# Row maxima of the segment attention: whole masked rows on VectorE in place of packed blocks

## The chip, the cores and the metric

One NeuronCore of a Trainium2 chip runs the whole program. The metric is device time in microseconds (us), the median of three runs. The engines work side by side: TensorE (PE in the profile; its weight loads are PEld), VectorE (DVE), ScalarE (ACT), GpSimd (POOL) and SyncE (SP, which here only issues transfers).

## The reference, cut to what matters

Two attention layers of 32 heads with 16 dimensions read the same 2048 tokens, and a gate mixes them. Side A is full softmax attention. Side B works on four segments of 512 tokens: causal softmax inside a segment, plus a memory carried from segment to segment. The change is in side B's softmax, in the row maxima that keep the exponential in range:

```python
def _A_ref(x, wqkv, wo):
    ...
    scores = jnp.einsum("bhqd,bhkd->bhqk", q, k) * scale
    p = _softmax(scores, axis=-1)
    o = jnp.einsum("bhqk,bhkd->bhqd", p, v)
    ...
def _B_ref(x, wq, wk, wv, wo, beta):
    B, S, D = x.shape
    H = 32; Dh = D // H; N = 4; L = S // N
    ...
    mask = (lambda x, dt: x.astype(dt))(ar[:, None] < ar[None, :], x.dtype) * (-1e9)
    ...
    for s in range(N):
        qs, ks, vs = q[:, :, s], k[:, :, s], v[:, :, s]
        logits = jnp.einsum("bhqd,bhkd->bhqk", qs, ks) * scale + mask
        p = _softmax(logits, axis=-1)
        a_dot = jnp.einsum("bhqk,bhkd->bhqd", p, vs)
        ...
```

## The kernel before

**Units.** The work of both sides is cut into units of four heads and 512 queries: 32 units of side A and 32 of side B (`NU`). A unit passes twice through TensorE. The first pass (`max_part`, products at L208) computes scores with queries in the partitions, and VectorE takes the maximum of each row. The second pass (`score_part`, products at L660) computes them again with keys in the partitions, with two extra rows of the query tile that carry the negated maximum, so that ScalarE can take the exponential straight from PSUM (L683, L680) and TensorE can multiply by the values (L716).

**Slots.** A unit of side A has 64 slots, one of side B 10 (`SLOTS`). Units alternate, so that a unit of A and one of B, 74 slots together, form the period of the kernel's middle stage. The loop at the end of `gated_mix` makes one slot after another, and this order is the order of each engine's queue. In slot n it emits one second-pass product and its exponential, and one first-pass bank for slot m = n + 96 (`LEAD`). After every third slot (`BURST`) it emits up to five pieces of value products, or eight small products of the output projection, so TensorE's stream comes in bursts: three score products, three first-pass banks, then the values. In the list `maxs` the ten B banks stand seven slots apart among the 64 of A; in the first block with B, and in the last one, which has two units of B, they stand three apart.

**Banks.** The first pass uses four PSUM banks of 128 x 512 in turn. TensorE can write a bank again when whoever read it is done, so it can be at most four slots ahead of its readers. The second pass has three banks (`st_ps`), and the values one.

**First pass of side A.** One product of 48 x 128 by 48 x 512 fills a bank, and one VectorE reduction of 128 x 512 empties it (L223). When the unit is complete, a small reduction joins the parts and negates them (L180).

**First pass of side B.** Queries 128 s to 128 s + 127 need keys 0 to 128 s + 127, the last 128 of these under the causal triangle. The kernel cuts these rows into blocks of 128 keys and packs the blocks so that each of the ten banks of a unit is full, in five kinds for each pair of heads. Kinds 0 and 1 hold four diagonal blocks each (four products of 128 columns): ScalarE copies the bank to SBUF (L234), GpSimd masks the copy (L235), and eight slots later VectorE reduces it (L238; `MASK_T`). Kinds 2 and 3 hold the rest of rows 1 and 3 of one head (products of 128 and 384 columns, reduction at L244), kind 4 the rest of row 2 of two heads (two products of 256, reduction at L248). That is 28 products and ten reductions of 512 columns for a unit. The block maxima go to a tile `pmB` that GpSimd filled with -3.0e38 once (L172 to L174), and a small reduction joins them (L182).

**After the maxima.** `finish_max` (L176) splits the negated maxima on GpSimd into two parts (L187, L188). `transpose_max` (L191) then transposes them on TensorE with four small products (L196), in a bank of the second pass; ScalarE copies the result (L199), and SyncE issues two transfers for each unit into the query tiles (L202). `todo` and `late` hold these steps back by fixed numbers of slots: for side B the small reduction comes 9 slots after the unit's last bank and the transposition 18 slots after it, for side A 0 and 14. Where both are due together, they share one transposition.

**Beside it.** GpSimd also masks the exponentials of side B (L664) and scales finished heads (L779, L781). VectorE also takes reciprocals of the softmax sums (L767) and multiplies them by gates (L769, L771). Ahead of the middle stage lies the projection of queries, keys and values; VectorE's product with a running sum at L467 is there.

Of the kernel before, what the change touches and what calls it, by code (L numbers as in the profile page):

```python
# [10 lines left out]
F32 = mybir.dt.float32  # L11
F32R = mybir.dt.float32r
AF = mybir.ActivationFunctionType
ALU = mybir.AluOpType
AX = mybir.AxisListType
# [7 lines left out]
CH = 512  # L23
NCH = S // CH
KT = D // 128
NG = 8
NO = 4
SCALE = 0.25
MASKED = -1.0e9 / SCALE

# [5 lines left out]
MOST = 3  # L38
NP = 6
GAP = {"A": 3, "B": 5}  # L40
MASK_T = 8
LATE_T = 8
PRE = 20
NKA, NKB = 8, 2
# [3 lines left out]
def gated_mix(ctx, tc, x, xT, wqkv, a_wo, b_wq, b_wk, b_wv, b_wo, beta, gate_w, out):  # L48
    nc = tc.nc
# [7 lines left out]
    for side in "AB":  # L57
        for o in range(NO):
            for c in range(NCH):
# [20 lines left out]
                            compare_op=ALU.not_equal, fill=1.0)  # L80
# [12 lines left out]
    mp = ctx.enter_context(tc.tile_pool(name="mp", bufs=2))  # L93
# [18 lines left out]
    for k in range(NU):  # L112
        mine = {u: iter(range(32)) for u in range(2)}
# [3 lines left out]
        for p in range(64 + 10 * len(bs)):  # L117
            r = (len(maxs) + 1) % 2
            i = (p - start) // apart
# [42 lines left out]
    def rows(t, h, n):  # L162

        return t[64 * (h // 2):64 * (h // 2) + n, h % 2]


    pmt = {}
    todo = []
    late = []


    pmB = [mp.tile([128, 2, 4, 8], F32, name=f"pmB{i}", bufs=1) for i in range(2)]  # L172
    for t in pmB:
        nc.gpsimd.memset(t, -3.0e38)  # L174

    def finish_max(u):  # L176
        nm = mp.tile([128, 4, 4], F32, tag="nm", name="nm")
        pm = pmt.pop(u)
        if u[0] == "A":
            nc.vector.tensor_reduce(nm, pm, axis=AX.X, op=ALU.max, negate=True)  # L180
        else:
            nc.vector.tensor_reduce(nm.rearrange("p h (a b) -> p (h a) b", b=2),  # L182
                                    pm.rearrange("p b h (a k) -> p (h a) b k", a=2), axis=AX.X, op=ALU.max, negate=True)

        ms = mp.tile([128, 2, 2, 2, 4], F32R, tag="ms", name="ms")
        nv = nm.rearrange("p (r h) s -> p r h s", r=2)
        nc.gpsimd.tensor_copy(ms[:, :, 0], nv)  # L187
        nc.gpsimd.tensor_sub(ms[:, :, 1], nv, ms[:, :, 0].bitcast(F32))  # L188
        return ms
# [11 lines left out]
            for r in range(2):  # L201
                nc.sync.dma_start(raw(qt[u])[64 * r + 48:64 * r + 50], raw(mt)[32 * i + 16 * r:32 * i + 16 * r + 16])  # L202

    def blocked(ps):
        return ps.rearrange("p (b t) -> p b t", t=128)

    def max_product(ps, u, h, s, n0, n, k, k0=0):
        nc.tensor.matmul(ps[:, n0:n0 + n], rows(qt[u][:, :, s * 128:(s + 1) * 128], h, 48), rows(k[:, :, k0:k0 + n], h, 48),  # L208
                         start=True, stop=True)

    def max_part(m, bank):

        u, (r, i) = maxs[m]
        side, g, c = u
        if u not in pmt:
            pmt[u] = mp.tile([128, 4, 4, 4], F32, tag="pmA", name="pm") if side == "A" else pmB[(c * NG + g) % 2]
        pm = pmt[u]
        ps = bank()
        if side == "A":

            kc, s, h = i // 8, i % 8 // 2, 2 * r + i % 2
            max_product(ps, u, h, s, 0, CH, kt_[u, kc])
            nc.vector.tensor_reduce(pm[:, h, s, kc:kc + 1], ps, axis=AX.X, op=ALU.max)  # L223
        else:


            k = kt_[u, c]
            h0 = 2 * r
            if i < 2:
                for n in range(4):  # L230
                    b = i + 2 * (n % 2)
                    max_product(ps, u, h0 + n // 2, b, 128 * n, 128, k, 128 * b)
                dg = dp.tile([128, 4, 128], F32, tag="dg", name="dg")
                nc.scalar.copy(dg, blocked(ps))  # L234
                nc.gpsimd.affine_select(out=dg, in_=dg, pattern=[[0, 4], [-1, 128]], base=0, channel_multiplier=1,  # L235
                                        compare_op=ALU.is_ge, fill=MASKED)
                to = pm[:, i, h0:h0 + 2, 3::4] if i == 0 else pm[:, i, h0:h0 + 2, 1::6]
                todo.append((m + MASK_T, lambda: nc.vector.tensor_reduce(  # L238
                    to, dg.rearrange("p (h s) t -> p h s t", h=2), axis=AX.X, op=ALU.max)))
            elif i < 4:  # L240
                h = h0 + i - 2
                max_product(ps, u, h, 1, 0, 128, k)
                max_product(ps, u, h, 3, 128, 384, k)
                nc.vector.tensor_reduce(pm[:, 1, h, 3:7], blocked(ps), axis=AX.X, op=ALU.max)  # L244
            else:
                for f in range(2):
                    max_product(ps, u, h0 + f, 2, 256 * f, 256, k)
                nc.vector.tensor_reduce(pm[:, 0, h0:h0 + 2, 4:6], ps.rearrange("p (h b t) -> p h b t", h=2, b=2), axis=AX.X,  # L248
                                        op=ALU.max)
        if m == last_max[u]:  # L250
            def finish():
                late.append((m + MASK_T + 2 + LATE_T - (4 if side == "A" else 0), u, finish_max(u)))
            todo.append((m + (MASK_T + 1 if side == "B" else 0), finish))

    def run_todo(m):

# [26 lines left out]
    with ExitStack() as p0:  # L283
# [264 lines left out]
        def some_max():  # L548
            m = mnext[0]
            if m == LEAD:  # L550
                return
            loads(m + 3 + PRE)
            for i in range(4):
                max_part(m + i, lambda: me_sm.tile([128, CH], F32, tag="sm", name="sm"))
            run_todo(m + 3)
            mnext[0] += 4
            run_late(me_ps, "me", mnext[0])
# [42 lines left out]
    pp = ctx.enter_context(tc.tile_pool(name="pp", bufs=NP, reuse_waits="tile"))  # L600

    va = ctx.enter_context(tc.tile_pool(name="va", bufs=2, reuse_waits="tile"))
    dp = ctx.enter_context(tc.tile_pool(name="dp", bufs=3, reuse_waits="tile"))
    ob = ctx.enter_context(tc.tile_pool(name="ob", bufs=2, reuse_waits="tile"))
    wo = ctx.enter_context(tc.tile_pool(name="wo", bufs=1, reuse_waits="tile"))
    fr = ctx.enter_context(tc.tile_pool(name="fr", bufs=1, reuse_waits="tile"))
# [28 lines left out]
    for (s, c), t in gate.items():  # L635
        nc.gpsimd.dma_start(t, gd["AB".index(s), c * CH:(c + 1) * CH].rearrange("(q t) -> q t", q=16)
                            .unsqueeze(0).broadcast_to([8, 16, 32]))

    pt_ = {}
    order_p = {}  # L640
# [159 lines left out]
    fill = []  # L800
# [63 lines left out]
    n = 0  # L864
    while n < nS or queue or beside or filled[0] < len(fill):
# [4 lines left out]
        m = n + LEAD  # L870
        if m < nS:
            loads(m + PRE)

            def bank():
                i = free.pop(0)
                free.append(i)
                return banks[i]
            max_part(m, bank)
# [22 lines left out]
    for b in range(4):  # L901
# [3 lines left out]
        t = fr.tile([128, D], F32, tag="vM" if b % 2 else "res", name="res", bufs=2)  # L905
# [4 lines left out]
def build():  # L910
    import concourse.bacc as bacc
    nc = bacc.Bacc("TRN2", target_bir_lowering=False, num_devices=1)
    shapes = {"x": (S, D), "xT": (D, S), "wqkv": (D, 3 * D), "a_wo": (D, D), "b_wq": (D, D), "b_wk": (D, D),
              "b_wv": (D, D), "b_wo": (D, D), "beta": (H,), "gate_w": (D,)}
    args = [nc.dram_tensor(n, s, F32, kind="ExternalInput").ap() for n, s in shapes.items()]
    out = nc.dram_tensor("out", (S, D), F32, kind="ExternalOutput").ap()
    with tile.TileContext(nc) as tc:
        gated_mix(tc, *args, out)
    return nc
# [23 lines left out]
```

## Time and profile before

| | us |
|---|---|
| Median of three runs (lowest to highest) | 1882.79 (1882.19 to 1883.36) |
| The profiled execution's own time | 1883.44 |
| Its span, first to last instruction | 1881.7 |
| Busy in the span: ACT | 1502.9 |
| Busy in the span: POOL | 314.9 |

The profile is of one execution. Its page gives the busy time of each engine and the chain of work that ended last. Views of the trace group instructions by line and shape, list them in order of time, and sum busy time in chosen stretches. "Busy" counts the time in which at least one instruction of the engine was under way, so overlapping instructions count once; the distance from one start to the next tells what an instruction costs its engine in a full queue. Matmul ends are modelled, so a busy TensorE is not the same as one at its peak.

### The profile page before, as it was taken

To read this page: it belongs to the slowest core of one execution; us is meant where nothing else is said; L and a number is where in the kernel's file an instruction comes from. 1 tells how busy PE (TensorE), PEld (TensorE's weight loads), DVE (VectorE), ACT (ScalarE), POOL (GpSimd) and SP (SyncE) were. 2 spreads that over 40 slices of the span, in tenths; PEclk is the share of its full clock that TensorE was granted. 3 is DMA by queue.
4 is the path that set the end of the run, shared out by engine and by line. 5 is a ranking of instruction groups with operands and counts; after the bars stand their busy time and mean duration, and the time that the engine had idled before them with its cause. 6 is when DMAs were issued, how large, how long until landed. Compare 5 with 4: busy or idle time off the path is not lost.

```text
span 1881.7 us, 46459 instructions
## 1 busy us (share of the span) xinstructions
PE 1863.1 (99%) x18153; PEld 1006.1 (53%) x18153; DVE 1596.5 (85%) x2745; ACT 1502.9 (80%) x2900; POOL 314.9 (17%) x515
## 2 busy tenths in 40 slices
PE   9999999999999999999999999999999999999998
PEld 7888676555555454444444444444444454555545
DVE  4235777999999999999999999999999999999820
ACT  5445444898888898888888888888888888888884
POOL 3001222111111111121111111211121211111210
PEclk9999999999999999999999999999999999999999
DMA  7567555234343433343434343434343434343211
GB/s 239 192 231 255 196 184 192 84 115 136 87 109 86 115 91 111 94 117 97 117 92 117 98 113 102 113 98 113 97 113 101 113 103 115 102 114 95 84 57 46
DMA packets 124170, 227.31 MB, mean 121 GB/s; under 512 B 34952, under 2 KB 49960, under 8 KB 123440
## 3 DMA queue, kind: packets, MB, share of 16 engines
q1 hardware_dynamic: 122448, 222.68, 41.1%
q8 instruction: 144, 2.36, 0.5%
q0 software_dynamic: 1216, 1.14, 0.2%
q14 instruction: 74, 0.61, 0.1%
q10 hardware_dynamic: 288, 0.52, 0.1%
HBM read 155.52 MB, written 67.52 MB: 119 GB/s over the span
## 4 chain that ended last, share of the span: by engine, by line
PE 90%; ACT 4%; DMA 3%; DVE 1%; issue 1%; SPq 1%; POOL 1%; ACTq 0%; POOLq 0%; DVEq 0%
PE ops L716 30%; PE st L660 27%; PE sm L208 14%; PE pr L320 11%; PE ops L793 6%; ACT p L683 2%; ACT dg L234 1%; DMA qB<-mt 1%; PE num L502 1%; POOL mn L380 1%; SPq L202 0%; DMA qdB<-q 0%; PE sm L793 0%; PE mps L533 0%; DMA raw<-wqkv 0%
## 5 line engine op out<-in xcount | busy, mean ns | idle before, releaser
L683 ACT ACTIVATE p<-st 128x512 f32<-128x512 f32 x2304 | 1223.4, 605 | 180.8 <-PE sm L208 147.4
L223 DVE TENSOR_REDUCE pm<-sm 128x1 f32<-128x512 f32 x2048 | 1282.9, 683 | 62.1 <-PE sm L208 43.0
L208 PE MATMUL sm<-kA,qA 48*128 48x512 f32 x2048 | 741.5, 445 | 0.0
L660 PE MATMUL st<-qA,kA 50*128 50x512 f32 x2048 | 693.6, 436 | 3.6 <-ACT p L683 3.1
L660 PEld LDWEIGHTS st<-qA,kA 50*128 50x128 f32 x2048 | 332.9, 185 | 436.0 <-ACT p L683 370.6
L716 PE MATMUL ops<-p,vA 128*17 128x512 f32 (+3 forms) x5848 | 556.4, 469 | 0.0
L208 PEld LDWEIGHTS sm<-kA,qA 48*128 48x128 f32 x2048 | 332.5, 184 | 21.1 <-DVE pm L223 7.9
L716 PEld LDWEIGHTS ops<-p,vA 128*17 128x17 f32 x5848 | 109.7, 95 | 174.0 <-issue 152.4
L208 PE MATMUL sm<-kB,qB 48*128 48x128 f32 (+2 forms) x896 | 168.6, 291 | 0.0
L208 PEld LDWEIGHTS sm<-kB,qB 48*128 48x128 f32 x896 | 134.6, 186 | 9.8 <-DVE pm L223 2.8
L235 POOL TENSOR_SCALAR_AFFINE_SELECT dg<-dg 128x512 f32<-128x512 f32 x128 | 81.2, 635 | 289.1 <-ACT dg L234 289.1
L660 PE MATMUL st<-qB,kB 50*128 50x384 f32 (+3 forms) x512 | 120.4, 341 | 2.6 <-DMA qB<-mt 1.2
L187 POOL CAST ms<-nm 128x16 fp32r<-128x16 f32 x64 | 12.6, 196 | 646.6 <-DVE nm L180 401.5
L383 DVE TENSOR_TENSOR q<-full,q 128x512 fp32r<-128x512 f32 x64 | 44.1, 689 | 86.9 <-ACT q L376 86.4
L660 PEld LDWEIGHTS st<-qB,kB 50*128 50x128 f32 x512 | 71.4, 185 | 67.9 <-ACT p L683 47.3
L664 POOL TENSOR_SCALAR_AFFINE_SELECT p<-p 128x512 f32<-128x512 f32 x128 | 78.8, 634 | 95.9 <-ACT p L683 93.9
L244 DVE TENSOR_REDUCE pmB<-sm 128x4 f32<-128x512 f32 x128 | 87.3, 682 | 0.5 <-PE sm L208 0.5
L716 PE MATMUL ops<-p,vB 128*17 128x128 f32 (+3 forms) x1192 | 86.5, 398 | 0.4
L238 DVE TENSOR_REDUCE pmB<-dg 128x4 f32<-128x512 f32 x128 | 86.7, 677 | 0.0
L375 ACT COPY full<-pr 128x512 f32<-128x512 f32 x64 | 37.3, 583 | 52.0 <-PE pr L320 51.8
L234 ACT COPY dg<-sm 128x512 f32<-128x512 f32 x128 | 76.4, 597 | 1.0 <-DVE pmB L238 0.6
L767 DVE RECIPROCAL rec<-rec 128x32 f32<-128x32 f32 x44 | 15.1, 344 | 66.0 <-DMA rec<-odA 35.3
(145 smaller groups left out, 1588.8 us busy)
## 6 DMA issues: line engine op xcount, KB each, us to landing
kA<-kdA SPq DMA_DIRECT2D x256, 128.0 KB
vA<-vdA SPq DMA_DIRECT2D x31, 544.0 KB
kA<-kdA SPq DMA_DIRECT2D x256, 64.0 KB
qdA<-q SPq DMA_DIRECT2D x32, 256.0 KB
kdA<-q SPq DMA_DIRECT2D x32, 256.0 KB
qdB<-q SPq DMA_DIRECT2D x32, 256.0 KB
qA<-qdA SPq DMA_DIRECT2D x64, 128.0 KB
kdB<-q SPq DMA_DIRECT2D x32, 256.0 KB
```

The source lines that it names most:

```text
L208: nc.tensor.matmul(ps[:, n0:n0 + n], rows(qt[u][:, :, s * 128:(s + 1) * 128], h, 48), rows(k[:, :, k0:k0 + n], h, 48), start=True, stop=True)
L223: nc.vector.tensor_reduce(pm[:, h, s, kc:kc + 1], ps, axis=AX.X, op=ALU.max)
L234: nc.scalar.copy(dg, blocked(ps))
L235: nc.gpsimd.affine_select(out=dg, in_=dg, pattern=[[0, 4], [-1, 128]], base=0, channel_multiplier=1, compare_op=ALU.is_ge, fill=MASKED)
L238: todo.append((m + MASK_T, lambda: nc.vector.tensor_reduce(to, dg.rearrange("p (h s) t -> p h s t", h=2), axis=AX.X, op=ALU.max)))
L244: nc.vector.tensor_reduce(pm[:, 1, h, 3:7], blocked(ps), axis=AX.X, op=ALU.max)
L320: nc.tensor.matmul(ps, l(a, k), r(b, k), start=(n == 0), stop=(n == 11))
L660: nc.tensor.matmul(ps[:, n0:n0 + CH - q0], rows(k[:, :, b * 128:(b + 1) * 128], h, 50), rows(q[:, :, q0:], h, 50), start=True, stop=True)
L664: nc.gpsimd.affine_select(out=x, in_=x, pattern=[[0, 4], [1, 128]], base=0, channel_multiplier=-1, compare_op=ALU.is_ge, fill=0.0)
L683: nc.scalar.activation(p[:, h], ps, AF.Exp, scale=SCALE)
L716: nc.tensor.matmul(ops[32 * h:32 * h + 17, q0:q0 + 128 * w], v[:, 17 * h:17 * h + 17], p[:, h, c0:c0 + 128 * w], start=(i == 0), stop=done ...
L793: nc.tensor.matmul(ps[32 * t:32 * t + 32, 128 * (j % (ps.shape[1] // 128)):128 * (j % (ps.shape[1] // 128)) + 128], held[side, c][:, o, 12 ...
```

## The change

Each row of side B now stays whole. Row s of a head is one product with 128 (s + 1) columns. The eight rows of a pair of heads fill five banks: 128 + 384, 256 + 256, 128 + 384, 512 and 512 columns, so that a unit has 16 products in its ten banks. All products of a bank come first. Then VectorE runs one instruction per row: it adds a constant tile to the row (zero, and -3.0e38 above the diagonal of the last 128 columns), negates it, and takes the minimum over the row into one column of the unit's maxima. The sum itself goes to a scrap tile, `rest`, of which there is one. ScalarE's copies, GpSimd's masks and the delayed reductions of side B are gone, and so is its small reduction at the end. The constant tile is built once by GpSimd at the start of the middle stage. The transposition of a finished unit comes 12 slots after its last bank for side B and 8 for side A.

```diff
-MASK_T = 8
...
     def finish_max(u):
-        nm = mp.tile([128, 4, 4], F32, tag="nm", name="nm")
-        pm = pmt.pop(u)
+        nm = pmt.pop(u)
         if u[0] == "A":
+            pm, nm = nm, mp.tile([128, 4, 4], F32, tag="nm", name="nm")
             nc.vector.tensor_reduce(nm, pm, axis=AX.X, op=ALU.max, negate=True)
-        else:
-            nc.vector.tensor_reduce(nm.rearrange("p h (a b) -> p (h a) b", b=2),
-                                    pm.rearrange("p b h (a k) -> p (h a) b k", a=2), axis=AX.X, op=ALU.max, negate=True)
...
-            pmt[u] = mp.tile([128, 4, 4, 4], F32, tag="pmA", name="pm") if side == "A" else pmB[(c * NG + g) % 2]
+            pmt[u] = mp.tile([128, 4, 4] + [4] * (side == "A"), F32, tag="pm" + side, name="pm")
...
-            h0 = 2 * r
-            if i < 2:
-                for n in range(4):
-                    b = i + 2 * (n % 2)
-                    max_product(ps, u, h0 + n // 2, b, 128 * n, 128, k, 128 * b)
-                dg = dp.tile([128, 4, 128], F32, tag="dg", name="dg")
-                nc.scalar.copy(dg, blocked(ps))
-                nc.gpsimd.affine_select(out=dg, in_=dg, pattern=[[0, 4], [-1, 128]], base=0, channel_multiplier=1,
-                                        compare_op=ALU.is_ge, fill=MASKED)
-                to = pm[:, i, h0:h0 + 2, 3::4] if i == 0 else pm[:, i, h0:h0 + 2, 1::6]
-                todo.append((m + MASK_T, lambda: nc.vector.tensor_reduce(
-                    to, dg.rearrange("p (h s) t -> p h s t", h=2), axis=AX.X, op=ALU.max)))
-            elif i < 4:
-                h = h0 + i - 2
-                max_product(ps, u, h, 1, 0, 128, k)
-                max_product(ps, u, h, 3, 128, 384, k)
-                nc.vector.tensor_reduce(pm[:, 1, h, 3:7], blocked(ps), axis=AX.X, op=ALU.max)
-            else:
-                for f in range(2):
-                    max_product(ps, u, h0 + f, 2, 256 * f, 256, k)
-                nc.vector.tensor_reduce(pm[:, 0, h0:h0 + 2, 4:6], ps.rearrange("p (h b t) -> p h b t", h=2, b=2), axis=AX.X,
-                                        op=ALU.max)
+            mine = [(2 * r + h, s, 128 * (s == 2) + 256 * (s == 1 and h), 128 * (s + 1))
+                    for h, s in (((0, 0), (0, 2)), ((0, 1), (1, 1)), ((1, 0), (1, 2)), ((0, 3),), ((1, 3),))[i]]
+            for h, s, n0, w in mine:
+                max_product(ps, u, h, s, n0, w, k)
+            for h, s, n0, w in mine:
+                nc.vector.tensor_tensor_reduce(out=tri["rest"][:, 0:w], in0=ps[:, n0:n0 + w], in1=tri["mask"][:, CH - w:],
+                                               scale=-1.0, scalar=3.0e38, op0=ALU.add, op1=ALU.min,
+                                               accum_out=pm[:, h, s:s + 1])
         if m == last_max[u]:
             def finish():
-                late.append((m + MASK_T + 2 + LATE_T - (4 if side == "A" else 0), u, finish_max(u)))
-            todo.append((m + (MASK_T + 1 if side == "B" else 0), finish))
+                late.append((m + LATE_T + (4 if side == "B" else 0), u, finish_max(u)))
+            todo.append((m, finish))
...
-    dp = ctx.enter_context(tc.tile_pool(name="dp", bufs=3, reuse_waits="tile"))
+    dp = ctx.enter_context(tc.tile_pool(name="dp", bufs=1, reuse_waits="tile"))
...
+    tri["rest"] = dp.tile([128, CH], F32, name="rest")
+    tri["mask"] = dp.tile([128, CH], F32, name="mask")
+    nc.gpsimd.memset(tri["mask"], 0.0)
+    nc.gpsimd.affine_select(out=tri["mask"][:, 384:], in_=tri["mask"][:, 384:], pattern=[[-1, 128]], base=0, channel_multiplier=1,
+                            compare_op=ALU.is_ge, fill=-3.0e38)
```

More of the change, by code (lines that the diff above doesn't have):

```diff
@@ L28 @@
 SCALE = 0.25
-MASKED = -1.0e9 / SCALE
 SLOTS = {"A": 64, "B": 10}
@@ L167, in gated_mix @@
     pmt = {}
+    tri = {}
     todo = []
     late = []
-    pmB = [mp.tile([128, 2, 4, 8], F32, name=f"pmB{i}", bufs=1) for i in range(2)]
-    for t in pmB:
-        nc.gpsimd.memset(t, -3.0e38)
     def finish_max(u):
-        nm = mp.tile([128, 4, 4], F32, tag="nm", name="nm")
-        pm = pmt.pop(u)
+        nm = pmt.pop(u)
         if u[0] == "A":
+            pm, nm = nm, mp.tile([128, 4, 4], F32, tag="nm", name="nm")
             nc.vector.tensor_reduce(nm, pm, axis=AX.X, op=ALU.max, negate=True)
-        else:
-            nc.vector.tensor_reduce(nm.rearrange("p h (a b) -> p (h a) b", b=2),
-                                    pm.rearrange("p b h (a k) -> p (h a) b k", a=2), axis=AX.X, op=ALU.max, negate=True)
         ms = mp.tile([128, 2, 2, 2, 4], F32R, tag="ms", name="ms")
@@ L202, in transpose_max @@
                 nc.sync.dma_start(raw(qt[u])[64 * r + 48:64 * r + 50], raw(mt)[32 * i + 16 * r:32 * i + 16 * r + 16])
-    def blocked(ps):
-        return ps.rearrange("p (b t) -> p b t", t=128)
     def max_product(ps, u, h, s, n0, n, k, k0=0):
```

## The prediction, made before the changed kernel ran

> **What bounds the kernel now.** I read the page first, then busy time by stretches, then the order of time inside the middle stage.
>
> ```profile
> PE 1863.1 (99%) x18153; PEld 1006.1 (53%) x18153; DVE 1596.5 (85%) x2745; ACT 1502.9 (80%) x2900; POOL 314.9 (17%) x515
> PE 90%; ACT 4%; DMA 3%; DVE 1%; issue 1%; SPq 1%; POOL 1%; ACTq 0%; POOLq 0%; DVEq 0%
> ```
>
> TensorE is busy nearly throughout and is 90% of the chain that ended last. VectorE's 85% mixes stages with different limits, so the next view cuts the span into the projection, the middle stage (its first part, twenty periods of 74 slots, its last part) and the tail. Columns: stretch, length, then busy us (instructions) of PE, PEld, DVE, ACT, POOL, the clock, DMA. The last two rows are the same view for the line of the reciprocals (L767) and for the small reduction that ends a unit of B (L182).
>
> ```profile
> 328.00:551.00 223.00, 221.96 (x2240) 114.50 (x2238) 216.38 (x370) 197.59 (x388) 32.46 (x61) 1.00 0.39 109
> 551.00:1503.00 952.00, 945.77 (x9475) 446.71 (x9478) 921.84 (x1577) 837.01 (x1638) 161.76 (x276) 1.00 0.40 104
> 1503.00:1800.00 297.00, 295.05 (x3697) 154.57 (x3689) 278.47 (x473) 256.68 (x503) 52.16 (x89) 1.00 0.36 99
> 551.00:1503.00 952.00, 4.18 (x20) 1.00 0.40 104
> 551.00:1503.00 952.00, 9.60 (x28) 1.00 0.40 104
> ```
>
> Twenty units of B end in 952 us, so a period is 47.6 us. VectorE is busy 921.84 of 952, so it is idle only 1.5 us in a period. The stage from 328 to 1800 us is 1472 / 47.6 = 30.9 periods, and all 32 units of B have their first pass in it.
>
> What VectorE must do in a period, from its order of time (start, length, line, count):
>
> ```profile
> 853.08 3.67 DVE L223 TENSOR_REDUCE pm<-sm 128x1 f32<-128x512 f32 x6
> 856.66 0.68 DVE L244 TENSOR_REDUCE pmB<-sm 128x4 f32<-128x512 f32 x1
> ...
> 873.12 0.22 DVE L180 TENSOR_REDUCE nm<-pm 128x16 f32<-128x64 f32 x1
> 873.26 3.07 DVE L223 TENSOR_REDUCE pm<-sm 128x1 f32<-128x512 f32 x5
> 876.25 0.21 DVE L182 TENSOR_REDUCE nm<-pmB 128x16 f32<-128x64 f32 x1
> 876.37 1.28 DVE L223 TENSOR_REDUCE pm<-sm 128x1 f32<-128x512 f32 x2
> ...
> 1188.21 0.34 DVE L767 RECIPROCAL rec<-rec 128x32 f32<-128x32 f32 x1
> 1188.58 0.19 DVE L771 TENSOR_TENSOR rec<-rec,gA 128x32 f32<-128x32 f32 x1
> 1188.69 3.07 DVE L223 TENSOR_REDUCE pm<-sm 128x1 f32<-128x512 f32 x5
> ```
>
> Six reductions take 856.66 - 853.08 = 3.58 us from start to start, 0.598 each, although one alone lasts 0.68: neighbours overlap. The two small reductions cost 0.14 and 0.12, a reciprocal with its gate 1188.69 - 1188.21 = 0.48, and there are 28 / 20 = 1.4 of those in a period. VectorE's floor is 74 x 0.598 + 0.26 + 1.4 x 0.48 = 45.2 us of 47.6: 2.4 us of room.
>
> TensorE, in bursts (each row is the first score product of a burst, or its values):
>
> ```profile
> 854.82 0.49 PE L660 MATMUL st<-qA,kA 50*128 50x512 f32 x1
> 856.32 0.50 PE L660 MATMUL st<-qA,kA 50*128 50x512 f32 x1
> 858.44 0.49 PE L660 MATMUL st<-qA,kA 50*128 50x512 f32 x1
> ...
> 873.62 0.50 PE L660 MATMUL st<-qA,kA 50*128 50x512 f32 x1
> 874.53 1.05 PE L716 MATMUL ops<-p,vA 128*17 128x512 f32 x8
> 875.51 0.49 PE L660 MATMUL st<-qA,kA 50*128 50x512 f32 x1
> 876.61 1.05 PE L716 MATMUL ops<-p,vA 128*17 128x512 f32 x8
> 877.60 0.50 PE L660 MATMUL st<-qA,kA 50*128 50x512 f32 x1
> ```
>
> The plain burst at 873.62 lasts 1.89, against 3 x 0.598 = 1.79 on VectorE: TensorE sets the pace. The next one, with a bank of four small products, lasts 2.09. The bursts at 854.82 and 856.32 last 1.50 and 2.12, together 3.62 for six banks, 0.603 a bank, which is VectorE's rate; in just that time VectorE ran without a break (853.08 to past 856.66). So TensorE paces most bursts, and VectorE paces where a burst with few values would let TensorE run ahead.
>
> **The change, part by part.** The built program has 512 first-pass products of B where there were 896, in the same 320 banks with the same columns.
>
> *TensorE.* Four banks of a unit lose three products each (four of 128 columns become one of 512); the two banks of 128 + 384 for each pair of heads and the one of 256 + 256 remain, under other numbers. A bank of four costs 2.09 - 1.89 = 0.20 us more than a whole one where TensorE paces, and nothing where VectorE does. Bounds are 0 and 0.8 a unit; I take three of four banks, 0.6, as most bursts are paced by TensorE. The period on TensorE becomes 47.6 - 0.6 = 47.0.
>
> *VectorE, removed.* Ten reductions and L182, 10 x 0.598 + 0.12 = 6.1 us a unit.
>
> *VectorE, added.* Sixteen masked instructions over 5120 columns, each with a read-out of its accumulator. No such instruction is in this trace. The nearest is L467, which also has two sources and a sum read out:
>
> ```profile
> 303.96 0.68 DVE L467 SCALAR_TENSOR_TENSOR jk<-xg,gw 128x512 f32<-128x512 f32 x1
> 304.57 0.08 DVE L467 DVE_READ_ACCUMULATOR jk<-xg,gw 128x1 f32 x1
> 304.69 0.69 DVE L467 SCALAR_TENSOR_TENSOR jk<-xg,gw 128x512 f32<-128x512 f32 x1
> 305.30 0.08 DVE L467 DVE_READ_ACCUMULATOR jk<-xg,gw 128x1 f32 x1
> 305.30 0.68 DVE L223 TENSOR_REDUCE pm<-sm 128x1 f32<-128x512 f32 x1
> ...
> L542 DVE TENSOR_TENSOR mrun<-mps,mrun 128x136 f32<-128x136 f32 x8 | 2.3, 293 | 0.0
> L392 DVE SCALAR_TENSOR_TENSOR ph<-full,ex 128x512 f32<-128x512 f32 x24 | 16.6, 690 | 13.9 <-ACT ex L387 13.9
> ```
>
> From L542 (PSUM and SBUF sources) and L392, 376 columns more take 690 - 293 = 397 ns, so 1.056 ns a column and 0.15 us fixed when an instruction stands alone. In a full queue the fixed part is 0.598 - 512 x 1.056 / 1000 = 0.06; with the read-out it is the same, since the reduction behind L467 starts 0.61 after it, together with the read-out. But L467 behind L467, which writes the same scrap tile, starts 0.73 after it: it waits for its neighbour to end (304.64) and starts 0.05 later. In the changed kernel the second row of a bank has just this wait, for `rest`; behind it queue the reductions of A, and behind those TensorE's banks. So a bank of two rows costs 0.285 + 0.05 for 128 columns alone, then 0.405 + 0.06 for 384, together 0.80; 256 + 256 comes to 0.42 + 0.05 + 0.27 + 0.06 = 0.80 as well; a single row 0.61. A unit has six such pairs and four single rows: 6 x 0.80 + 4 x 0.61 = 7.2 us, 1.1 more than before. VectorE's floor becomes 45.2 + 1.1 = 46.3 of TensorE's 47.0.
>
> Bounds: with no wait exposed and 0.06 each, 5.41 + 16 x 0.06 = 6.4, +0.3 a unit. With each instruction standing alone (0.15), its read-out (0.08) and a wait (0.05), 5.41 + 16 x 0.28 = 9.9, +3.8. I keep 7.2, by L467, the nearest row.
>
> The Trainium skill ("VectorE: DVE Perf Modes", The DRAIN you can't avoid) says that chained VectorE instructions cost the same with or without a semaphore between them. By it the second row of a bank would not pay its wait, some 0.13 us, and a unit would add 0.3 to 0.4 us instead of 1.1. The trace speaks against it: 0.73 between the two L467, 0.61 ahead of the reduction that waits for no neighbour.
>
> *ScalarE and GpSimd.*
>
> ```profile
> L234 ACT COPY dg<-sm 128x512 f32<-128x512 f32 x128 | 76.4, 597 | 1.0 <-DVE pmB L238 0.6 <-PE st L660 0.4
> L235 POOL TENSOR_SCALAR_AFFINE_SELECT dg<-dg 128x512 f32<-128x512 f32 x128 | 81.2, 635 | 289.1 <-ACT dg L234 289.1
> PEld st L660 <- ACT dg L234: 21.4, 36, 0.9
> ...
> PEld sm L208 <- DVE pm L223: 10.7, 46, 0.4
> ```
>
> Four copies a unit, 2.4 us, leave ScalarE; behind them queue exponentials, and TensorE's weight loads for the second pass were seen waiting behind a copy for 21.4 us in all (third row: total, times, longest; the last row has what it waited for VectorE's release of a bank). Most of it lies under value products still running. I take 0, with 0.5 us a period as the other bound, and VectorE's nearness is what hides it. GpSimd's 81 us free no one: the masked copies were reduced eight slots later. The constant tile costs one or two us once, ahead of the first bank of B, where GpSimd waits anyway.
>
> *Transpositions six slots earlier*, with ScalarE's copy and four issues of SyncE:
>
> ```profile
> 876.87 0.22 POOL L188 TENSOR_TENSOR ms<-nm,ms 128x16 fp32r<-128x16 f32 x1
> 877.04 1.28 POOL L779 TENSOR_TENSOR vM<-vM,inv 128x512 f32<-128x512 f32 x1
> ...
> 881.50 0.39 PE L196 MATMUL mt_ps<-identf,ms 128*32 128x128 f32 x4
> ```
>
> Six slots are 6 x 47.6 / 74 = 3.9 us, so this transposition moves from 881.50 to 877.6. A's maxima were joined at 873.34 and B's, no longer held back, come earlier, so GpSimd has 3.9 us or so where it needs 0.6 (876.25 + 0.21 to 876.87 + 0.22). If its queue held two scalings of 1.28 just then, some 0.7 us would still be left. I take 0. The transfers into the query rows are issued 3.9 us earlier too; SyncE's later key loads merely change places with them, and B's first scores, which cost little by waiting, gain nothing that I count.
>
> *The sum.* TensorE 47.0, VectorE 46.3, so VectorE is at 98.5%. The seven slots from one pair bank to the next still fit (6 x 0.598 + 0.80 = 4.39 on VectorE against 7 x 1.89 / 3 = 4.41 on TensorE), but a pair bank that falls among short bursts costs its whole 0.2; I count one a period. 47.2 in place of 47.6: -0.4 x 30.9 = -12 us. From the profiled execution's own 1883.4 (span 1881.7 and 1.7 around it) this gives 1871; that execution is 0.7 above the median shown, which I leave in the rounding.
>
> **The rivals.**
>
> *VectorE becomes the pace (slower).* Place: the pair banks. It decides once a unit adds more than the 2.4 us of room, that is when the fixed cost of a masked instruction passes (6.1 + 2.4 - 5.41) / 16 = 0.19 us; my working has (7.2 - 5.41) / 16 = 0.11, and the upper bound 0.28. At 0.24 a unit takes 9.25, +3.1; the floor is 48.3, with 0.2 of coupling 48.5, +0.9 x 30.9 = +28: 1911. At the upper bound 49.2: 1933. For it: VectorE has already 97% of the stretch, and the instruction is not in the trace. Against: L467 is at 0.07 to 0.19.
>
> *VectorE takes what TensorE gives (no change).* If the one-pair coupling is two or three pairs, 47.5 to 47.7: 1880 to 1886. For it: the bursts at 854.82 and 856.32.
>
> *More is freed.* All four banks (0.8) and ScalarE's 0.5 show: TensorE 46.3, VectorE 46.3, coupling 0.2: 46.5, -34: 1849. Against: both engines would have to be full together.
>
> *Half rate.* If two sources and an accumulator ran at half the rate, a unit would add another 5.41 us: floor 51.7, +4.1 x 30.9 = +127: 2010. L467 with two sources and a sum takes 0.68 for 512 columns, as L392 without a sum, so nothing here bears it out. The Trainium skill states such a halving for two SBUF sources that are not bf16 ("Vector Engine (DVE) Microarchitecture Reference", Points that are easy to get wrong); L467 has just these sources and disagrees.
>
> *The change doesn't do what it says.* The program has the 512 products and 512 masked instructions, so I give this nothing.
>
> **How the numbers follow.** Forecast 1871 (own range 1858 to 1879) 0.37; more freed 0.12; no change 0.14; VectorE the pace 0.34; half rate 0.03. Faster by over 0.2% (below 1879, about what a measurement of this kernel can tell): 0.37 + 0.12 = 0.49. Within it 0.14. Slower 0.34 + 0.03 = 0.37. The range runs from the freed case, 1849, to the price of VectorE as the pace, 1911, and leaves out some 0.2 beyond both.
>
> **What would show it.** Right: bursts with one product of 512 last 1.89; pairs of masked rows cost VectorE 0.80 to the next start; its idle time in twenty periods shrinks from 30 us to about 15 or less, and TensorE's waits for VectorE grow from their 10.7 us. Wrong: a masked instruction of 128 columns lasting much over 0.29, a read-out that holds the next reduction, or TensorE idle behind VectorE in every burst with a pair. The prediction falls if a period is above 47.6.

## The result, and the profile after

The changed kernel takes 1857.57 us (median of four runs, 1856.77 to 1859.19), the kernel before 1882.65 us beside it. The ratio is 0.9868, with a 95% interval of 0.985 to 0.9885: about 25 us faster. The forecast was 12 us faster, at 1871; the direction was right, the size half of what came.

The page after the change has these rows where the one before was quoted:

```profile
PE 1846.4 (100%) x17769; PEld 987.1 (53%) x17769; DVE 1609.3 (87%) x3417; ACT 1446.3 (78%) x2772; POOL 236.6 (13%) x387
PE 94%; DVE 2%; DMA 1%; ACT 1%; POOL 1%; issue 0%; SPq 0%; POOLq 0%; DVEq 0%
```

VectorE is busy longer than before, 1609.3 us against 1596.5, in a shorter span; ScalarE's and GpSimd's copies and masks are gone. In the chain, ScalarE's share fell from 4% to 1%.

Busy time by the same stretches of the middle stage (length, then busy us of PE, PEld, DVE, ACT, POOL, the clock, DMA):

```profile
328.00:551.00 223.00, 222.78 (x2188) 116.40 (x2188) 220.19 (x480) 190.73 (x369) 19.26 (x40) 1.00 0.40 110
551.00:1503.00 952.00, 952.00 (x9457) 443.01 (x9451) 944.11 (x2034) 814.18 (x1583) 114.89 (x200) 1.00 0.41 106
1503.00:1800.00 297.00, 296.97 (x3694) 150.84 (x3694) 265.61 (x582) 252.45 (x495) 38.02 (x66) 1.00 0.36 99
```

VectorE is idle 8 us of the 952 where it was idle 30, and TensorE, which had 6 us without a matmul, now has none.

The length of a period comes from the order of time, by the transposition of finished units, which comes once a period; first the changed kernel, then the one before:

```profile
547.55 0.39 PE L187 MATMUL mt_ps<-identf,ms 128*32 128x128 f32 x4
...
1483.49 0.28 PE L187 MATMUL mt_ps<-identf,ms 128*32 128x128 f32 x2
```

```profile
551.74 0.39 PE L196 MATMUL mt_ps<-identf,ms 128*32 128x128 f32 x4
...
1503.50 0.28 PE L196 MATMUL mt_ps<-identf,ms 128*32 128x128 f32 x2
```

Twenty periods took 951.76 and take 935.94 us: 47.6 and 46.8 a period. The prediction had 47.2.

What the new instruction costs VectorE, from the changed kernel's order of time:

```profile
869.45 3.67 DVE L211 TENSOR_REDUCE pm<-sm 128x1 f32<-128x512 f32 x6
873.03 0.28 DVE L221 CUSTOM_DVE_ANT_0 rest<-sm,mask 128x128 f32<-128x128 f32 x1
873.24 0.08 DVE L221 DVE_READ_ACCUMULATOR2_ANT pm<- 128x1 f32 x1
873.36 0.56 DVE L221 CUSTOM_DVE_ANT_0 rest<-sm,mask 128x384 f32<-128x384 f32 x1
873.84 0.08 DVE L221 DVE_READ_ACCUMULATOR2_ANT pm<- 128x1 f32 x1
873.84 3.68 DVE L211 TENSOR_REDUCE pm<-sm 128x1 f32<-128x512 f32 x6
```

The pair of rows takes 873.84 - 873.03 = 0.81 from its start to that of the next reduction. The second row starts 0.12 after the first one's read-out began, where the reduction behind it starts together with the read-out: that is the wait for the scrap tile. The groups by shape give one instruction's mean (last but one number group: busy us, mean ns):

```profile
L221 DVE CUSTOM_DVE_ANT_0 rest<-sm,mask 128x512 f32<-128x512 f32 x128 | 87.2, 681 | 0.5 <-PE sm L196 0.4
L221 DVE CUSTOM_DVE_ANT_0 rest<-sm,mask 128x384 f32<-128x384 f32 x128 | 71.4, 558 | 4.4
L221 DVE CUSTOM_DVE_ANT_0 rest<-sm,mask 128x256 f32<-128x256 f32 x128 | 53.7, 420 | 2.2
L221 DVE CUSTOM_DVE_ANT_0 rest<-sm,mask 128x128 f32<-128x128 f32 x128 | 36.0, 281 | 0.4 <-PE sm L196 0.4
```

From 128 to 512 columns the time grows by 400 ns, 1.04 ns a column, about the 1.056 of L392 and L542, and some 0.15 us fixed when one stands alone, as the prediction had it.

TensorE's bursts, by their first score products, with the one first-pass product of B in the burst at 812.94:

```profile
811.05 0.49 PE L640 MATMUL st<-qA,kA 50*128 50x512 f32 x1
...
812.94 0.50 PE L640 MATMUL st<-qA,kA 50*128 50x512 f32 x1
...
813.51 0.39 PE L196 MATMUL sm<-kB,qB 48*128 48x512 f32 x1
814.81 0.50 PE L640 MATMUL st<-qA,kA 50*128 50x512 f32 x1
```

The burst with a whole row of B lasts 814.81 - 812.94 = 1.87, as the plain one ahead of it (1.89). A bank of four products had made it 2.09.

Where did the rest come from? The chain of waits, cut to the twenty periods and summed by line, first before and then after:

```profile
by line: PE ops L716 37.2%; PE st L660 32.5%; PE sm L208 16.9%; PE ops L793 6.9%; ACT p L683 2.6%; issue 1.0%; ACT dg L234 0.9%; DMA qB<-mt 0.8%; SPq L202 0.6%; ACT oraw L720 0.3%; PE mt_ps L196 0.3%; ACT mt L199 0.1%; ACTq L199 0.0%; ACTq 
```

```profile
by line: PE ops L696 39.6%; PE st L640 34.8%; PE sm L196 18.0%; PE ops L773 7.2%; PE mt_ps L187 0.4%; issue 0.0%
```

Before, the exponentials (2.6%) and the copies (0.9%) held 3.5% of the chain in this stretch, 33 us of 952; the transfers into the query rows had another 1.4%. After, all of it is TensorE. A share of the chain is not yet what removing its work is worth: the copies came to 28 us in the whole kernel (e5_no_copy below). One such detour in the kernel before, in order of time:

```profile
693.88 0.43 PE st L660
694.31 0.05 PE sm L208
694.36 0.25 ACT p L683
694.61 0.23 issue
694.84 0.59 ACT p L683
695.43 0.48 ACT dg L234
695.91 0.51 ACT p L683
696.42 0.03 issue
696.45 0.47 PE st L660
```

From 694.36 to 696.45 the chain runs on ScalarE: two exponentials, the copy of a diagonal bank, one more exponential, and only then can TensorE write the next score bank. The prediction had costed these copies at nothing. Which part of the 25 us belongs to the products, which to the copies and what VectorE's longer work took back, a trace does not tell; the experiments do.

### The profile page after: what moved, and what is told of

It is laid out like the page before. It is cut to its first block, busy times and chain, and to the rows that moved or that the text cites. A ratio compares the mean times of both kernels' runs of the same rounds, so it can differ in the third digit from the quotient of the medians.

```text
span 1855.0 us, 45914 instructions
## 1 busy us (share of the span) xinstructions
PE 1846.4 (100%) x17769; PEld 987.1 (53%) x17769; DVE 1609.3 (87%) x3417; ACT 1446.3 (78%) x2772; POOL 236.6 (13%) x387
## 4 chain that ended last, share of the span: by engine, by line
PE 94%; DVE 2%; DMA 1%; ACT 1%; POOL 1%; issue 0%; SPq 0%; POOLq 0%; DVEq 0%
PE ops L696 32%; PE st L640 28%; PE sm L196 15%; PE pr L294 11%; PE ops L773 6%; PE sm L773 1%; DVE pm L211 1%; POOL mn L354 1%; PE num L476 1%; DMA raw<-xT 0%; PE mt_ps L187 0%; DMA qdB<-q 0%; PE mps L507 0%; DMA raw<-wqkv 0%; ACT ex L361 0%
## 5 line engine op out<-in xcount | busy, mean ns | idle before, releaser
L663 ACT ACTIVATE p<-st 128x512 f32<-128x512 f32 x2304 | 1210.8, 601 | 207.0 <-PE sm L196 164.4
L211 DVE TENSOR_REDUCE pm<-sm 128x1 f32<-128x512 f32 x2048 | 1264.5, 682 | 14.3 <-PE sm L196 13.7
L640 PE MATMUL st<-qA,kA 50*128 50x512 f32 x2048 | 678.8, 433 | 0.0
L221 DVE CUSTOM_DVE_ANT_0 rest<-sm,mask 128x128 f32<-128x128 f32 (+3 forms) x512 | 248.3, 485 | 7.5 <-PE sm L196 0.8
L196 PE MATMUL sm<-kB,qB 48*128 48x128 f32 (+3 forms) x512 | 149.3, 352 | 0.0
L640 PE MATMUL st<-qB,kB 50*128 50x384 f32 (+3 forms) x512 | 114.1, 337 | 0.0
L196 PEld LDWEIGHTS sm<-kB,qB 48*128 48x128 f32 x512 | 86.1, 185 | 7.3 <-DVE pm L211 2.9
L773 PE MATMUL ops<-woA,vA 128*32 128x128 f32 x1664 | 66.9, 278 | 0.0
L773 PE MATMUL ops<-woB,vB 128*32 128x128 f32 x1664 | 64.6, 273 | 0.0
L294 PE MATMUL pr<-xh,wql 128*128 128x512 f32 x128 | 54.4, 425 | 0.3 <-ACT xh L407 0.2
```

The lines of the kernel that those rows point to most:

```text
L221: nc.vector.tensor_tensor_reduce(out=tri["rest"][:, 0:w], in0=ps[:, n0:n0 + w], in1=tri["mask"][:, CH - w:], scale=-1.0, scalar=3.0e38, op ...
L294: nc.tensor.matmul(ps, l(a, k), r(b, k), start=(n == 0), stop=(n == 11))
L640: nc.tensor.matmul(ps[:, n0:n0 + CH - q0], rows(k[:, :, b * 128:(b + 1) * 128], h, 50), rows(q[:, :, q0:], h, 50), start=True, stop=True)
L663: nc.scalar.activation(p[:, h], ps, AF.Exp, scale=SCALE)
L773: nc.tensor.matmul(ps[32 * t:32 * t + 32, 128 * (j % (ps.shape[1] // 128)):128 * (j % (ps.shape[1] // 128)) + 128], held[side, c][:, o, 12 ...
```

## The experiments

Each kernel is compared with runs of the kernel before on the same chip. Those runs' medians lay between 1882.98 and 1883.84 us. "The changed kernel" means 1857.6. A difference between two of these kernels can be off by about 1 us, as these medians are.

**The products put back (e1_split).** In the changed kernel, the rows of 512 columns are made of four products:

```diff
             for h, s, n0, w in mine:
-                max_product(ps, u, h, s, n0, w, k)
+                for b in range(0, w, 128 if w == CH else w):
+                    max_product(ps, u, h, s, n0 + b, 128 if w == CH else w, k, b)
```

> The changed kernel, with its four whole rows of 512 columns per unit made of four products of 128 columns each, so 28 products a unit again; VectorE, ScalarE and GpSimd as in the changed kernel (1857.6 us). Theory P, the fewer products are what paid: a bank of four costs TensorE 0.20 us more than a whole one, 0.8 us a unit, so most of the gain goes: 1872 to 1882. Theory C, ScalarE's copies are what paid: TensorE has room for them beside VectorE, 1857 to 1861. Both in equal parts: 1864 to 1870.

Measured: 1869.97 us, ratio 0.9928 (0.9914 to 0.9943). Between the two theories, at the upper end of "equal parts": 12.4 us, half of the gain, when the products are put back alone. A burst with such a bank, from this kernel's order of time:

```profile
813.40 0.50 PE L641 MATMUL st<-qA,kA 50*128 50x512 f32 x1
...
813.98 0.55 PE L196 MATMUL sm<-kB,qB 48*128 48x128 f32 x4
815.45 0.49 PE L641 MATMUL st<-qA,kA 50*128 50x512 f32 x1
```

It lasts 2.05 where a plain one lasts 1.89. Four such banks in 31 periods would be 20 to 25 us at full price; 12.4 came, so some were hidden behind VectorE.

**ScalarE's work put back (e2_act).** Four copies a unit that wait for nothing and that nobody waits for:

```diff
                 max_product(ps, u, h, s, n0, w, k)
+            if i < 2:
+                nc.scalar.copy(tri["spare"], tri["mask"])
```

> The changed kernel plus four ScalarE copies of 128x512 a unit, in the slots where the kernel before had them, from the constant tile to a scrap tile that nobody reads; no bank waits for them. Theory C, the copies delayed exponentials and so TensorE: up to 0.5 us a period comes back, 1867 to 1874. Theory P: 1857 to 1860.

Measured: 1872.65 us, ratio 0.9942 (0.9927 to 0.9956). ScalarE's time alone costs 15.1 us, although ScalarE is not the busiest engine. Its busy time in the twenty periods' stretch, and the chain there by line:

```profile
551.00:1503.00 952.00, 942.69 (x9283) 421.03 (x9275) 939.54 (x2012) 841.21 (x1648) 112.07 (x196) 1.00 0.40 105
```

```profile
by line: PE ops L699 36.0%; PE st L643 33.1%; PE sm L196 13.7%; ACT p L666 7.2%; PE ops L776 6.2%; ACT spare L221 2.1%; issue 0.9%; ACT oraw L703 0.6%; PE mt_ps L187 0.2%; ACTq L190 0.0%
```

ScalarE is busy 841 of 952 us, 88%, and with that the exponentials are back on the chain, with 7.2%, and TensorE has 9 us without a matmul again.

**The transposition where it was (e3_late).**

```diff
-                late.append((m + LATE_T + (4 if side == "B" else 0), u, finish_max(u)))
+                late.append((m + 6 + LATE_T + (4 if side == "B" else 0), u, finish_max(u)))
```

> The changed kernel with the transpositions of finished units six slots later, where the kernel before had them. Theory T, the earlier transposition paid, since transfers into the query rows no longer arrive late for the first scores of side B: 1860 to 1865. Otherwise 1856 to 1859.

Measured: 1858.35 us, ratio 0.9869 (0.9853 to 0.9886), the changed kernel's within the noise. In the changed kernel the earlier transfers, which had 1.4% of the chain before, bought nothing. In a kernel with less work on VectorE they may; see e7_both.

**Two scrap tiles (e4_two_rest).**

```diff
-            for h, s, n0, w in mine:
-                nc.vector.tensor_tensor_reduce(out=tri["rest"][:, 0:w], in0=ps[:, n0:n0 + w], in1=tri["mask"][:, CH - w:],
+            for f, (h, s, n0, w) in enumerate(mine):
+                nc.vector.tensor_tensor_reduce(out=tri["rest", f][:, 0:w], in0=ps[:, n0:n0 + w], in1=tri["mask"][:, CH - w:],
```

> The changed kernel with two scrap tiles in turn, so that the second row of a bank no longer waits for the first one: VectorE gets 6 x 0.13 = 0.8 us a unit back. Theory V, VectorE is now the pace of every period (46.8 us against a floor of 46.3 from its starts): 1857.6 - 0.8 x 31 = 1833, or wherever TensorE's own floor stops it, 1833 to 1850. Theory B, TensorE still paces and VectorE is only full because it waits half-started: 1855 to 1859.

Measured: 1843.63 us, ratio 0.979 (0.9775 to 0.9804): 14 us faster than the changed kernel and the fastest kernel of this study. The pair of rows in its order of time:

```profile
840.84 0.28 DVE L221 CUSTOM_DVE_ANT_0 rest<-sm,mask 128x128 f32<-128x128 f32 x1
841.05 0.08 DVE L221 DVE_READ_ACCUMULATOR2_ANT pm<- 128x1 f32 x1
841.05 0.55 DVE L221 CUSTOM_DVE_ANT_0 rest<-sm,mask 128x384 f32<-128x384 f32 x1
841.53 0.08 DVE L221 DVE_READ_ACCUMULATOR2_ANT pm<- 128x1 f32 x1
841.53 3.80 DVE L211 TENSOR_REDUCE pm<-sm 128x1 f32<-128x512 f32 x6
```

The second row now starts with the read-out of the first, 0.21 after its start and not 0.33, and the pair takes 0.69. VectorE got back 0.12 us in each of 192 pairs, 23 us in all, and 14 show: VectorE was the pace of the changed kernel in part, with TensorE close behind. The changed kernel's chain had shown nothing of this: it named TensorE alone, while VectorE was busy 944 of 952 us beside it. The Trainium skill measured that a semaphore after each of eight chained copies on VectorE costs nothing extra ("VectorE: DVE Perf Modes", The DRAIN you can't avoid). These rows differ: 0.33 us from start to start with the wait, 0.21 without it.

**The kernel before, without copies and masks (e5_no_copy).** VectorE reduces the diagonal banks from PSUM; the maxima run over masked keys too.

```diff
-                dg = dp.tile([128, 4, 128], F32, tag="dg", name="dg")
-                nc.scalar.copy(dg, blocked(ps))
-                nc.gpsimd.affine_select(out=dg, in_=dg, pattern=[[0, 4], [-1, 128]], base=0, channel_multiplier=1,
-                                        compare_op=ALU.is_ge, fill=MASKED)
...
-                todo.append((m + MASK_T, lambda: nc.vector.tensor_reduce(
-                    to, dg.rearrange("p (h s) t -> p h s t", h=2), axis=AX.X, op=ALU.max)))
+                nc.vector.tensor_reduce(to, ps.rearrange("p (h s t) -> p h s t", h=2, s=2), axis=AX.X, op=ALU.max)
```

> The kernel before, but VectorE reduces the diagonal banks straight from PSUM in their own slots: ScalarE's 128 copies and GpSimd's 128 masks are left out (so these maxima run over masked keys too); 28 products and ten VectorE reductions a unit as before. Theory C+P (copies cost 15 us, products 12, as put back into the changed kernel): 1866 to 1871. If the copies cost only where VectorE is full as in the changed kernel: 1878 to 1884.

Measured: 1855.1 us, ratio 0.9854 (0.9838 to 0.9871), below the range of the theory. With all 28 products left, doing without the copies and masks, with VectorE's reductions back in their banks' own slots, is worth 28 us, more than the whole change.

```profile
by line: PE ops L711 39.0%; PE st L655 34.8%; PE sm L208 16.8%; PE ops L788 7.4%; DMA qB<-mt 0.6%; SPq L202 0.5%; PE mt_ps L196 0.4%; issue 0.2%; ACT p L678 0.1%; ACT mt L199 0.0%
```

In its chain of the twenty periods' stretch the exponentials are down from 2.6% to 0.1%.

**The kernel before, with one product in each diagonal bank (e6_one_product).** Copies and masks stay; these banks hold other scores.

```diff
-                for n in range(4):
-                    b = i + 2 * (n % 2)
-                    max_product(ps, u, h0 + n // 2, b, 128 * n, 128, k, 128 * b)
+                max_product(ps, u, h0, i, 0, CH, k)
```

> The kernel before, with one product of 512 columns in each of the four diagonal banks of a unit in place of four of 128 (so these banks hold other scores): 16 products, copies and masks kept. Theory C+P: 12 us less, 1869 to 1874. If TensorE then only waits for exponentials held up by the copies: 1878 to 1883.

Measured: 1880.97 us, ratio 0.9987 (0.9978 to 0.9997), about 2 us. The theory of a plain sum falls here: with the copies in place, fewer products mostly let TensorE wait longer for the exponentials. In the chain of the same stretch these now hold 4.2%, where the kernel before has 2.6%:

```profile
by line: PE ops L714 36.8%; PE st L658 33.0%; PE sm L208 15.2%; PE ops L791 6.7%; ACT p L681 4.2%; ACT dg L232 1.1%; issue 1.0%; DMA qB<-mt 0.8%; SPq L202 0.7%; ACT oraw L718 0.3%; PE mt_ps L196 0.2%; ACT mt L199 0.1%; ACTq L199 0.0%; ACTq 
```

**Both edits on the kernel before (e7_both).** The two diffs above together.

> Both edits on the kernel before: no copies and masks, one product in each diagonal bank (so these maxima are of other scores), and VectorE still at ten reductions a unit, so without the change's 1.1 us a unit on VectorE. If the two gains add up and VectorE's extra work costs nothing: 1856 to 1858, as the changed kernel. If the changed kernel paid for VectorE's extra 1.1 us a unit: 1835 to 1848, the nearer to 1835 the more of it shows.

Measured: 1845.39 us, ratio 0.9802 (0.9788 to 0.9817). Without the copies the products are worth 1855.1 - 1845.4 = 10 us. The changed kernel has VectorE's 1.1 us more a unit and is 12 us slower; that is about the price of VectorE's longer work. It is not a clean price: here the transpositions still come late, and the transfers behind them hold 2.2% of the chain and SyncE's queue ahead of them 1.6%, of which the changed kernel has nothing:

```profile
by line: PE ops L709 37.9%; PE st L653 33.4%; PE sm L208 15.6%; PE ops L786 7.5%; DMA qB<-mt 2.2%; SPq L202 1.6%; ACT p L676 0.8%; issue 0.5%; PE mt_ps L196 0.4%; ACT mt L199 0.2%
```

The kernel with two scrap tiles, whose rows still cost VectorE 6 x 0.69 + 4 x 0.61 = 6.6 us a unit against 6.1 here, is even 2 us faster than this one. So VectorE's price may be above 12 us; no run separates the two.

**What of a copy costs (e8_idle_copy, e9_bank_copy).** Both start from the kernel without copies and masks (1855). The first adds ScalarE copies between two SBUF tiles, the second the copies from the banks, which nobody reads:

```diff
+                nc.scalar.copy(spare[1], spare[0])
                 nc.vector.tensor_reduce(to, ps.rearrange("p (h s t) -> p h s t", h=2, s=2), axis=AX.X, op=ALU.max)
```

```diff
+                dg = dp.tile([128, 4, 128], F32, tag="dg", name="dg")
+                nc.scalar.copy(dg, blocked(ps))
                 nc.vector.tensor_reduce(to, ps.rearrange("p (h s t) -> p h s t", h=2, s=2), axis=AX.X, op=ALU.max)
```

> The kernel without copies and masks (1855 us, maxima over masked keys too), plus the same number of ScalarE copies of 128x512 in the same slots, from one SBUF tile to another: ScalarE's time is back, but no copy waits for a product and no bank waits for a copy. Theory L (load): ScalarE's time in front of the exponentials is what the copies cost, 1870 to 1883. Theory W (wait): what cost was the copy that waits in ScalarE's queue for its product, or the bank that waits for the copy, 1854 to 1860.

> The same kernel without masks, with ScalarE's copies of the diagonal banks from PSUM back, though nobody reads the copies; VectorE reduces the banks from PSUM, so each bank waits for both. Theory L: as with the idle copies, within 3 us of them. Theory W: well above the idle copies, 1875 to 1884. If both stay near 1855 to 1862, neither copy nor wait is the cause, and what is left is VectorE's delayed reduction behind GpSimd's mask.

Measured: 1871.51 us (0.994; 0.9925 to 0.9954) and 1893.91 us (1.0058; 1.0043 to 1.0073). Idle copies cost 16.4 us, so ScalarE's time is more than half of the 28. Copies from the banks cost 22 us more than idle ones, above the ranges of both theories. But that run does not price the bank's wait: as it was built, VectorE's reduction of a diagonal bank starts only after ScalarE's copy of it. VectorE's waits in the twenty periods' stretch (total us, times, longest):

```profile
DVE pmB L236 <- ACT dg L235: 36.1, 73, 0.8
```

In the kernel before, VectorE never waits ahead of its delayed reduction.

**Idle copies where VectorE is not full (e10_act_two_rest).** The kernel with two scrap tiles, with the idle copies (to bf16, for space).

```diff
+            if i < 2:
+                nc.scalar.copy(tri["spare"], tri["mask"])
```

> The changed kernel with two scrap tiles (1843.6 us) plus four idle ScalarE copies a unit (to bf16). In the changed kernel they cost 15 us beside a full VectorE. Theory L, the price is ScalarE's own time in front of the exponentials: again 12 to 18, 1856 to 1862. If it came from ScalarE and VectorE being full together: 1844 to 1851.

Measured: 1866.39 us, ratio 0.9914 (0.9897 to 0.993): 22.8 us, over the range. The price of ScalarE's time does not come from a full VectorE; with VectorE relieved it shows in a greater part.

**The copies one slot later (e11_copy_later).** The kernel before, with

```diff
-                nc.scalar.copy(dg, blocked(ps))
-                nc.gpsimd.affine_select(out=dg, in_=dg, pattern=[[0, 4], [-1, 128]], base=0, channel_multiplier=1,
-                                        compare_op=ALU.is_ge, fill=MASKED)
+                def leave_bank(dg=dg, ps=ps):
+                    nc.scalar.copy(dg, blocked(ps))
+                    nc.gpsimd.affine_select(out=dg, in_=dg, pattern=[[0, 4], [-1, 128]], base=0, channel_multiplier=1,
+                                            compare_op=ALU.is_ge, fill=MASKED)
+                todo.append((m + 1, leave_bank))
```

> The kernel before with each of ScalarE's diagonal copies (and its mask) put one slot later in the queues, so that the copy stands behind one more exponential and its products are done when its turn comes; the bank is held longer. Of the 28 us that leaving the copies out gained, 16 came back with idle copies. Theory W, the other 12 are the copy waiting in ScalarE's queue for its four products: 1871 to 1877. Theory B, they are the bank that waits for the copy: later copies hold it longer, 1884 to 1892. If neither moves (1881 to 1884), the 12 us lie in VectorE's delayed reduction or elsewhere and stay open.

Measured: 1888.74 us, ratio 1.0028 (1.0018 to 1.0037). The copy's wait for its products is not the missing part: a later copy makes it worse, and in the kernel before ScalarE sat idle ahead of these copies for only 1.0 us in all (the row of L234). The time lies where theory B put it, but its trace hardly shows the bank's wait: first-pass products waited behind a copy for 0.8 us in all here, and not at all in the kernel before. Whether the 12 us beyond the idle copies are the bank held longer, VectorE's delayed reduction or GpSimd's masks, which no run leaves out alone, stays open.

## Why the prediction fell short, step by step

**VectorE's price was right.** A pair of masked rows takes 0.81 (forecast 0.80), single instructions 281 to 681 ns as worked out from L542 and L392, the wait for the scrap tile shows, and the read-out holds nobody. VectorE's idle time in the stretch fell to 8 us ("about 15 or less"), and TensorE's waits for VectorE's release of a bank grew from 10.7 to 13.9 us. Half rate is excluded by the row of 512 columns at 681 ns. (In the working's view by stretches the last two rows stand in the other order than its sentence says: x20 is L182, x28 is L767. The sum uses them rightly.)

**The products were over-sized.** Forecast 0.6 us a period, 19 us. Measured 12.4 us put back into the changed kernel and 10 us taken out of the kernel without copies, 0.3 to 0.4 a period: about half of the price of four such banks (0.8), where I took three quarters. On the kernel before alone they were worth only 2 us.

**The step that failed is "I take 0, with 0.5 us a period as the other bound, and VectorE's nearness is what hides it".** Leaving out copies and masks is worth 28 us on the kernel before, 28 / 31 = 0.9 us a period, beyond the bound; as mere ScalarE time, 15 to 23 us (0.5 to 0.7 a period). The other 12 or so stay open. The working went by a row of weight loads whose wait ended with a copy, 21.4 us in 36 times. But a copy delays the exponentials behind it, and in the chain that time stands under the exponential's name. The waits view cannot show it: its row for weight loads behind exponentials is no smaller without the copies (first the kernel before, then e5_no_copy, in the same stretch).

```profile
PEld st L660 <- ACT p L683: 281.4, 440, 0.9
PEld st L655 <- ACT p L678: 298.7, 497, 0.9
```

The chain's "ACT 4%" was on the page and was quoted; followed by line it would have shown exponentials and copies with 33 us in the twenty periods. And VectorE's nearness hid only a part: idle copies cost 15 us beside a full VectorE and 23 with VectorE relieved.

**The coupling was under-sized.** Forecast 0.2 us a period, 6 us, for VectorE's 1.1 us more a unit. The changed kernel is 12 us slower than the kernel with its products, without copies and with the old VectorE work: 0.4 a period, or more.

**The transposition was right at nothing** in the changed kernel: six slots later again changes under 1 us.

**The sum.** Forecast -19 + 0 + 6 = about -12. By the kernels: -28 for the copies and masks, -10 for the products behind them, +12 for the rest, VectorE above all, together -26. That this meets the measured -25 proves nothing: each of these kernels starts where the one before it ends, so the steps add up by construction. The two small errors did not cancel each other. The products were forecast some 9 us too good and the coupling 6 us too cheap, both towards a faster kernel, and so they made up for about half of the missing 28. With the measured sizes of both and nothing for the copies, the sum would have been about +2: that the direction came out right was luck. Of the rivals, "more is freed" had the right mechanism in ScalarE's share, but with the products' full price and at 1849. The slower rival's condition was not met: a masked instruction's fixed cost came out where L467 put it.

## What to carry to other kernels

Here an engine that was 88% busy and fed the bounding engine through a few buffers was not off the path: before costing such an engine's removed work at nothing, sum the chain by line in that stage, since work put ahead of the critical instructions shows under their names. The chain does not price it, and it does not name a second engine that is as full: for both it took a run. Gains on two engines do not add up one by one: the products alone gave 2 us, the copies and masks 28, both 38. And a scrap output that nobody reads can still order the instructions that write it; a second one cost 2 KB a partition and gave 14 us.

## What the runs showed of the hardware that was not expected

A VectorE instruction that writes the same scrap tile as its neighbour starts 0.12 us after the neighbour's read-out began, a wait that the prediction had from L467; with a tile of its own it starts together with it (873.36 against 873.24, and 841.05 against 841.05). The accumulator's read-out, 84 ns, costs the queue almost nothing by itself: the reduction behind it starts together with it (873.84). Idle ScalarE copies of 0.6 us, 80 us in all, cost three kernels bound by TensorE and VectorE 15 to 23 us.
